# A router phase's first operations ahead of the weight loads, and the low parts of w1 and w2 behind its one-hot

## The chip, the cores and the metric

The kernel runs on one core of a Trainium2 chip (trn2). The core has a matrix engine (TensorE, PE in the rows), VectorE (DVE), ScalarE (ACT), GpSimd (POOL) and a queue engine, SyncE (SP), which here only issues transfers; all five run their own instruction lists in order and wait for one another through semaphores. The metric is the device time of one execution in microseconds, here the median of three runs.

## What is computed

Three stages, in float32, of which the reference is (cut):

```python
for t in range(S):                                   # attention with decay, 4 x 8 heads, 768 steps, 48 wide
    state = alpha[:, :, t, :, None] * state + einsum('bhd,bhe->bhde', k[:, :, t], v[:, :, t])
    y[:, :, t] = einsum('bhd,bhde->bhe', q[:, :, t], state)
x = y.transpose(0, 2, 1, 3).reshape(3072, 384)

logits = x @ w_gate                                  # 8 experts, 384 tokens for each
for idx in argsort(-logits.flatten()):               # greedy: best pair first
    tok, e = idx // 8, idx % 8
    if assigned[tok] >= 0 or counts[e] >= 384: continue
    assigned[tok] = e; counts[e] += 1
for e in range(8):
    out[assigned == e] = relu(x[assigned == e] @ w1[e]) @ w2[e]      # 384 -> 1024 -> 384

g = out @ w_gate2                                    # 384 -> 1536
result = (g * sigmoid(g) * (out @ w_val)) @ w_out    # 1536 -> 384
```

## The kernel before

**Stages.** First the attention, in chunks of the 768 steps, which leaves x in DRAM (`xd`). Then the router and the experts, interleaved. The router runs in 8 phases (`Router.phase`): each searches a threshold by rounds of comparisons and counting matmuls, gives the tokens to their best expert that still has room, and closes one expert, whose token numbers `idx` and whose number `iw` it leaves. The experts are done in the order in which the phases close them: "expert 5" below is the sixth to be closed, by phase 5. For one expert's 384 tokens, `moe1` multiplies by w1 (`ph`, L758), takes the ReLU (`hT`, L759 and L760), and multiplies by w2 (`px`, L770); `moe2` makes gate and value (L788), their product `pp` (L795), its two parts `pTa`, `pTb` (L796 on ScalarE, L797 on GpSimd); `outp` multiplies by the output weights (`po`, L805, three groups of 36 matmuls), copies each out of PSUM (`o`, L808, ScalarE) and scatters it to the output rows (L809, an indirect transfer issued by GpSimd).

**Two halves of a number.** Each factor is kept as a high and a low float16 part, and a product is three matmuls. The weights of an expert come as float32 by a transfer on SP's queue into one of three buffers `stage` (`split`, L700). ScalarE writes the high part (L701). The low part of w1 is made by VectorE (L705). For w2 ScalarE first scales `stage` in place (L703) and GpSimd then subtracts (L704). A `stage` buffer is free for a next transfer when its low part is made. `loadw` does three loads of w1 and four of w2.

**The tokens of an expert.** `gather` issues three indirect transfers on GpSimd (L712), which fetch 128 rows of `xd` each by `idx`, and three transposing transfers on SP's queue (L720) that turn them into `xT`.

**PSUM.** `po`, `ph` and `px` share one pair of buffers (tag "pa"), so a group of L758 can only start when the group two before it has been copied out.

**The order.** The experts' code and the router's are generators. After each piece of expert work a counted time `now` goes forward, and `advance()` lets the current phase write its next step when `now` has come to `due`. When a phase is at its end, `advance()` calls `loads()`, which calls `loadw` for the expert that was just closed, and the next phase is begun at a later call. A phase's first operations after that are VectorE's: `pen` (L444, a penalty on full experts), `lp` (L447), the maximum `m` (L449), two passes for ties, the one-hot `oh_t` (L457), and the comparisons `cmp` (L527); six counting matmuls on TensorE (L532) read `oh_t` and `cmp`, VectorE's `cs` (L542) reads their sum, and one matmul (L545) reads `cs`. The phase's last are three matmuls (L618), then on VectorE `eq` (L621), two `et` (L623), `row` (L624) and `idx` (L626).

The Tile framework takes the instructions in the order in which the code writes them, estimates when each could run, and sets each engine's list by that. A call of `behind(x, y)` (`add_manual_dep` with no semaphore) keeps x behind y in that list where both are on one engine, and lets x's estimated time count from y's. Before the change, `pen` is held behind `idx` (`self.after`), and in `loadw` `lo` holds the low parts behind `idx` for expert 0 alone.

Of the kernel before, what the change touches and what calls it, by code (L numbers as in the profile page):

```python
# [356 lines left out]
class Router:  # L357
# [75 lines left out]
    def phase(self, i):  # L433
# [4 lines left out]
        bt=lambda a: a[:,None,:].to_broadcast([128,8,24])  # L438
# [12 lines left out]
        w=P2.tile([128,8,24],F32,name="w",tag="w",bufs=1)  # L451
        b=P2.tile([128,24],F32,name="bw")
# [1 line left out]
        v.tensor_tensor(w,w,be(self.w8),op=OP.mult)  # L454
        v.tensor_reduce(b,w.rearrange("p e t -> p t e"),axis=X,op=OP.max)
        oh=oh_t.rearrange("p t e -> p e t")
        v.tensor_tensor(oh,w,bt(b),op=OP.is_equal)  # L457
        if not first:
            mu=P2.tile([128,24],F32,name="mu")
            v.tensor_tensor(mu,m,self.ua,op=OP.add)  # L460
# [7 lines left out]
        else:  # L468
            lo,hi=yield from self.search(m,oh_t,i)
# [214 lines left out]
def ffn(ctx, tc, xd, w1, w2, M, MW, out, R, side):  # L684
# [11 lines left out]
    def split(dst,src,scale,dma_after=None,lo_after=None,pool=False):  # L696

        n,w=src.shape[0]//128,src.shape[1]
        s=ST.tile([128,1024],F32,name="stage",tag="stage",bufs=3)[:,:n*w].rearrange("p (a b) -> p a b",a=n)
        behind(nc.sync.dma_start(s,src.rearrange("(a p) b -> p a b",p=128)),dma_after)  # L700
        nc.scalar.activation(dst[0],s,AF.Copy,scale=scale)  # L701
        if pool:
            nc.scalar.activation(s,s,AF.Copy,scale=scale)  # L703
            behind(nc.gpsimd.tensor_tensor(dst[1],s,dst[0],op=OP.subtract),lo_after)  # L704
        else: behind(nc.vector.scalar_tensor_tensor(dst[1],s,scale,dst[0],op0=OP.mult,op1=OP.subtract),lo_after)  # L705
    xT={}; mm=R.mm
    id16=R.id16
    def gather(e):
        xT[e]=W2.tile([128,6,3,128],F16,name="xT")
        for j in range(3):  # L710
            r=W2.tile([128,2*DM],F16,name="rows",tag="rows",bufs=3)
            last=nc.gpsimd.indirect_dma_start(out=r,out_offset=None,in_=xr,in_offset=bass.IndirectOffsetOnAxis(ap=IDX[e][:,0,j:j+1],axis=0))  # L712
            if e==0 and XP0:

                pt=PT.tile([128,6,128],F16,name="ptx",tag=("pg","pg","pv")[j],bufs=2)
                for c in range(6): mm(pt[:,c],lhsT=r[:,c*128:(c+1)*128],rhs=id16,is_transpose=True,start=c==0,stop=c==5,skip_group_check=True)
                nc.vector.tensor_copy(xT[e][:,0:XA,j],pt[:,0:XA])
                if XA<6: nc.scalar.activation(xT[e][:,XA:6,j],pt[:,XA:6],AF.Copy)
            else:
                last=nc.sync.dma_start_transpose(xT[e][:,:,j],r)  # L720
        return last
    W={}
    def warm():

        ps=PT.tile([128,CAP],F32,name="warm",tag="pa",bufs=PA)
        for i in range(NW): behind(mm(ps,lhsT=R.own[:,0:128],rhs=R.own,start=True,stop=True),R.lastp)
    def loadw(e):
        if e==0 and NW: warm()
        a=W2.tile([128,2,3,F1],F16,name="w1s"); b=W2.tile([128,2,8,DM],F16,name="w2s")
        lo=R.after if e==0 else None  # L730
        if e==0 and GF: g=lo=gather(e)
        ex=nc.values_load(IW[e],engines=[mybir.EngineType.SP],min_val=0,max_val=E-1,skip_runtime_bounds_check_because="the router gives numbers of experts")
        wa=w1[bass.ds(ex,1)].rearrange("e d f -> (e d) f"); wb=w2[bass.ds(ex,1)].rearrange("e f d -> (e f) d")
        if e<WH:

            for h in range(2):
                c=slice(512*h,512*h+512)
                for k in (slice(0,2),slice(2,3)): split((a[:,0,k,c],a[:,1,k,c]),wa[k.start*128:k.stop*128,c],64.0,None,lo,WP[e]&1)
                if h==0 and not (e==0 and GF): g=gather(e)
        else:  # L740
            for k in range(3):
                split((a[:,0,k:k+1],a[:,1,k:k+1]),wa[k*128:k*128+128],64.0,None,lo,WP[e]&1)
            g=gather(e)
        if e: lo=g=None
        for k in range(4):
            split((b[:,0,2*k:2*k+2],b[:,1,2*k:2*k+2]),wb[k*256:k*256+256],64.0,g,lo,WP[e]&2)
        W[e]=(a,b)
# [64 lines left out]
    now=[0.0]; ph=[0]; cur=[R.phase(0)]; due=[0.0]; loaded=[0]; freed=[0]; avail={}; loaded_at=[]  # L812
    def loads():
        while loaded[0] in R.res and loaded[0]<freed[0]+2:
            i=loaded[0]; IDX[i],IW[i]=R.res[i]
            loadw(i); loaded[0]+=1; avail[i]=now[0]+GL; loaded_at.append(now[0])
    def advance():
        try: due[0]=now[0]+next(cur[0])
        except StopIteration:
            loads(); ph[0]+=1; cur[0]=R.phase(ph[0]) if ph[0]<E else None; due[0]=now[0]  # L820
    def run(g):

        t=next(g,None)
        if t is None: return False
        now[0]+=t
        while cur[0] is not None and due[0]<=now[0]: advance()
        for _ in range(CV): next(side,None)
        return True
    M.step=CS>0
    while ph[0]<1:  # L830
        advance()
        for _ in range(CS): next(side,None)
# [4 lines left out]
    while due[0]<=0: now[0]=due[0]; advance()  # L837
# [70 lines left out]
```

## Time and profile before

| | us |
|---|---|
| three runs | 1011.41, 1005.70, 1004.32 |
| median | 1005.7 |
| profiled execution | 1007.58 |
| its span | 1005.8 |
| TensorE busy | 835.2 (83%) |
| VectorE busy | 682.2 (68%) |
| ScalarE busy | 415.7 (41%) |
| GpSimd busy | 325.2 (32%) |
| mean granted TensorE clock, of 1 | 0.929 |

The span is cut by the page into 40 slices of 25.1 us; each digit is an engine's busy share in tenths, and PEclk is the granted TensorE clock in tenths:

```profile
PE   1577687967517679799899989989989997999997
DVE  8999989649798998657746865764775676232130
POOL 0434333436206443503412241350351236121231
PEclk9779799997758789899999999999999999999999
```

The attention takes some 13 slices, the router's first phase follows, and the experts take the rest, from about 350 us on. A time in a row counts from the start of the span. A row of a timeline merges neighbours of one kind; its length runs from the first's start to the last's end, and the bracket at its end is the idle time of the engine ahead of it with what ended it.

### The profile page before, as it was taken

What the parts mean: (1) busy time and instruction counts of PE and PEld (TensorE: products, weight loads), DVE (VectorE), ACT (ScalarE), POOL (GpSimd) and SP (SyncE); (2) the same over time, 40 slices, a digit from 0 to 9 for tenths busy, and PEclk for the clock granted to TensorE, in tenths of its full rate; (3) what the DMA queues carried; (4) which work ended last, traced back from release to release, by engine and by line L of the source; (5) the groups of instructions that cost most, each with busy time, mean ns of one, the idle gap of its engine ahead of it and who ended that gap; (6) DMA issues with size and microseconds to landing.
All of it is one profiled execution on the core that took longest, in us unless ns stands there. A gap on an engine that the chain in (4) does not pass through costs nothing. (4 is left out here: it accounts for less than half of the span.)

```text
span 1005.8 us, 18465 instructions
## 1 busy us (share of the span) xinstructions
PE 835.2 (83%) x7216; PEld 532.4 (53%) x7216; DVE 682.2 (68%) x1856; ACT 415.7 (41%) x768; POOL 325.2 (32%) x308
## 2 busy tenths in 40 slices
PE   1577687967517679799899989989989997999997
PEld 0356566756414345456556556645655653566664
DVE  8999989649798998657746865764775676232130
ACT  5637465865406453413422332251342245332130
POOL 0434333436206443503412241350351236121231
PEclk9779799997758789899999999999999999999999
DMA  9985999969416430600520240050050038100000
GB/s 190 166 130 98 189 178 143 178 121 199 118 42 194 127 102 5 192 1 1 152 46 1 95 103 2 30 167 1 1 174 23 1 119 226 26 1 1 24 1 24
DMA packets 144215, 90.28 MB, mean 90 GB/s; under 512 B 120960, under 2 KB 133760, under 8 KB 144128
## 3 DMA queue, kind: packets, MB, share of 16 engines
q1 hardware_dynamic: 141056, 79.67, 36.2%
q0 software_dynamic: 3072, 9.44, 2.9%
q8 instruction: 56, 0.92, 0.4%
q14 instruction: 31, 0.25, 0.1%
HBM read 62.94 MB, written 9.44 MB: 72 GB/s over the span
## 5 line engine op out<-in xcount | busy, mean ns | idle before, releaser
L797 POOL TENSOR_TENSOR pTa<-pp,pTa 128x384 f16<-128x384 f32 x64 | 59.5, 930 | 270.3 <-ACT pTa L796 267.0
L758 PE MATMUL ph<-xT,w1s 128*128 128x384 f16 x576 | 102.7, 334 | 16.1 <-DMA xT<-rows 6.7
L805 PE MATMUL po<-ma,pTa 128*128 128x384 f16 x576 | 108.9, 339 | 0.7 <-ACT pTa L796 0.7
L792 DVE TENSOR_TENSOR sg<-sg,pg 128x384 f32<-128x384 f32 x96 | 52.6, 548 | 77.7 <-ACT sg L791 77.7
L770 PE MATMUL px<-hT,w2s 128*128 128x384 f16 x576 | 99.7, 331 | 5.4 <-DVE hT L760 5.0
L758 PEld LDWEIGHTS <-w1s 128*128 128x128 f16 x576 | 55.9, 100 | 54.5 <-issue 21.0
L770 PEld LDWEIGHTS <-w2s 128*128 128x128 f16 x576 | 56.5, 99 | 43.9 <-issue 8.9
L805 PEld LDWEIGHTS <-pTa 128*128 128x128 f16 x576 | 57.2, 101 | 40.0 <-issue 5.7
L788 PEld LDWEIGHTS <-mb 128*128 128x128 f16 x576 | 55.7, 99 | 39.1 <-issue 4.1
L788 PEld LDWEIGHTS <-mc 128*128 128x128 f16 x576 | 55.6, 98 | 36.4 <-issue 0.2
L788 PEld LDWEIGHTS <-ma 128*128 128x128 f16 x576 | 55.4, 98 | 35.7
L791 ACT ACTIVATE sg<-pg 128x384 f32<-128x384 f32 x96 | 46.5, 484 | 55.0 <-PE pg L788 54.5
L796 ACT ACTIVATE pTa<-pp 128x384 f16<-128x384 f32 x64 | 33.3, 522 | 85.5 <-DVE pp L795 85.5
L795 DVE SCALAR_TENSOR_TENSOR pp<-sg,pv 128x384 f32<-128x384 f32 x96 | 52.8, 551 | 17.4 <-PE pv L788 12.2
L704 POOL TENSOR_TENSOR w2s<-stage,w2s 128x768 f16<-128x768 f32 x32 | 53.6, 1685 | 25.8 <-ACT stage L703 25.5
L797 POOL TENSOR_TENSOR pTb<-pp,pTb 128x384 f16<-128x384 f32 x32 | 33.3, 1042 | 86.8 <-ACT pTb L796 86.8
L788 PE MATMUL pg<-x,mb 128*128 128x384 f16 x288 | 59.2, 333 | 2.1 <-DVE x L773 1.2
L210 POOL TENSOR_TENSOR vh<-vx,vh 128x384 f16<-128x384 f32 x24 | 23.7, 990 | 106.1 <-ACT vh L209 73.2
L265 POOL TENSOR_TENSOR sBD<-st,sBD 48x384 f16<-48x384 f32 x46 | 48.0, 1044 | 30.6 <-ACT sBD L264 28.8
L788 PE MATMUL pv<-x,mb 128*128 128x384 f16 x288 | 57.4, 326 | 0.0
L161 DVE TENSOR_TENSOR FG<-FG,al 96x192 f32<-96x192 f32 x124 | 55.2, 453 | 2.4
L760 DVE SCALAR_TENSOR_TENSOR hT<-ph,hT 128x384 f16<-128x384 f32 x64 | 34.9, 546 | 28.6 <-ACT hT L759 28.6
(246 smaller groups left out, 1884.1 us busy)
## 6 DMA issues: line engine op xcount, KB each, us to landing
stage<-in_moe_w_dram SPq DMA_DIRECT2D x32, 384.0 KB, 3.6
stage<-in_moe_w_dram SPq DMA_DIRECT2D x23, 512.0 KB, 4.4
al<-in_alpha_dram SPq DMA_DIRECT2D x16, 288.0 KB, 6.1
qx<-in_q_dram SPq DMA_DIRECT2D x16, 288.0 KB, 9.3
kx<-in_k_dram SPq DMA_DIRECT2D x16, 288.0 KB, 11.4
vx<-in_v_dram SPq DMA_DIRECT2D x64, 72.0 KB, 3.3
xd<-xr SPq DMA_DIRECT2D x24, 192.0 KB, 3.5
words<-in_moe_w_gate_dram SPq DMA_DIRECT2D x9, 512.0 KB, 4.0
```

The source lines that it names most:

```text
L161: chain[p]=nc.vector.tensor_tensor(fg(j,HB-1-j),fg(j-1,HB-j),aa(j,HB-j),op=OP.mult)
L265: (nc.vector if n>=NG-ND else nc.gpsimd).tensor_tensor(sb[r,1,:,h,0:D],s[r],sb[r,0,:,h,0:D],op=OP.subtract)
L704: behind(nc.gpsimd.tensor_tensor(dst[1],s,dst[0],op=OP.subtract),lo_after)
L758: mm(ps,lhsT=a[:,l,k,f*128:(f+1)*128],rhs=x[:,r,k],start=i==0,stop=i==8); i+=1
L760: nc.vector.scalar_tensor_tensor(hT[:,1,f],ps,0.0,hT[:,0,f],op0=OP.max,op1=OP.subtract)
L770: mm(ps,lhsT=b[:,l,f,d*128:(d+1)*128],rhs=hT[:,r,f],start=i==0,stop=i==23); i+=1
L788: mm(ps,lhsT=w[:,l,k,f%4*128:(f%4+1)*128],rhs=x2[:,r,k],start=i==0,stop=i==8); i+=1
L791: nc.scalar.activation(sg,pg,AF.Sigmoid,scale=2.0**-16)
L792: nc.vector.tensor_tensor(sg,sg,pg,op=OP.mult)
L795: nc.vector.scalar_tensor_tensor(p,sg,2.0**-13,pv,op0=OP.mult,op1=OP.mult)
L797: nc.gpsimd.tensor_tensor(pT[e][f//4][:,1,f%4],p,pT[e][f//4][:,0,f%4],op=OP.subtract)
L805: mm(po,lhsT=pT[e][f//4][:,l,f%4,t*128:(t+1)*128],rhs=M.o[f//4][:,r,f%4],start=i==0,stop=i==35); i+=1
```

## The change

From the end of phase 1 on, `advance()` begins the next phase at once and writes its first step (`pen` to `oh_t`, and the first `cmp`) ahead of `loads()`. The operation that writes `oh_t` is kept as `self.best`, and for experts 1 to 6 the low parts of w1 and now of w2 too are held behind it in their engine's list; for expert 7 (no phase follows) by nothing. `e` 0 is as it was. Lines of the changed kernel stand one lower than before from L730 on (L758 is L759, L805 is L806, L808 is L809), and four lower behind `advance`.

```diff
--- before.py
+++ after.py
@@ -454,7 +454,7 @@
         v.tensor_tensor(w,w,be(self.w8),op=OP.mult)
         v.tensor_reduce(b,w.rearrange("p e t -> p t e"),axis=X,op=OP.max)
         oh=oh_t.rearrange("p t e -> p e t")
-        v.tensor_tensor(oh,w,bt(b),op=OP.is_equal)
+        self.best=v.tensor_tensor(oh,w,bt(b),op=OP.is_equal)
         if not first:
             mu=P2.tile([128,24],F32,name="mu")
             v.tensor_tensor(mu,m,self.ua,op=OP.add)
@@ -727,7 +727,8 @@
     def loadw(e):
         if e==0 and NW: warm()
         a=W2.tile([128,2,3,F1],F16,name="w1s"); b=W2.tile([128,2,8,DM],F16,name="w2s")
-        lo=R.after if e==0 else None
+
+        lo=R.after if e==0 else R.best if e<E-1 else None
         if e==0 and GF: g=lo=gather(e)
         ex=nc.values_load(IW[e],engines=[mybir.EngineType.SP],min_val=0,max_val=E-1,skip_runtime_bounds_check_because="the router gives numbers of experts")
         wa=w1[bass.ds(ex,1)].rearrange("e d f -> (e d) f"); wb=w2[bass.ds(ex,1)].rearrange("e f d -> (e f) d")
@@ -741,7 +742,7 @@
             for k in range(3):
                 split((a[:,0,k:k+1],a[:,1,k:k+1]),wa[k*128:k*128+128],64.0,None,lo,WP[e]&1)
             g=gather(e)
-        if e: lo=g=None
+        if e: g=None
         for k in range(4):
             split((b[:,0,2*k:2*k+2],b[:,1,2*k:2*k+2]),wb[k*256:k*256+256],64.0,g,lo,WP[e]&2)
         W[e]=(a,b)
@@ -817,7 +818,10 @@
     def advance():
         try: due[0]=now[0]+next(cur[0])
         except StopIteration:
-            loads(); ph[0]+=1; cur[0]=R.phase(ph[0]) if ph[0]<E else None; due[0]=now[0]
+            if ph[0]==0: loads()
+            ph[0]+=1; cur[0]=R.phase(ph[0]) if ph[0]<E else None; due[0]=now[0]
+            if cur[0] is not None and ph[0]>1: due[0]+=next(cur[0])
+            loads()
     def run(g):
 
         t=next(g,None)
```

**VectorE at expert 5**, from the last `pp` of expert 4 on. Names are those of the program; `r_` is a PSUM tile of the router. Before:

```order
L705 SCALAR_TENSOR_TENSOR w1s<-stage,w1s 128x1024
L621 TENSOR_TENSOR eq<-r_9791,q_4322 128x72
L623 TENSOR_TENSOR et<-eq,pay 128x72 x2
L705 SCALAR_TENSOR_TENSOR w1s<-stage,w1s 128x1024
L624 TENSOR_REDUCE row<-et 128x6
L705 SCALAR_TENSOR_TENSOR w1s<-stage,w1s 128x1024
L626 TENSOR_TENSOR idx<-row,r_9791 128x6
L444 TENSOR_SCALAR pen<-full 128x8
...
L457 TENSOR_TENSOR oh_t<-w,bw 128x8x24
L542 TENSOR_TENSOR cs<-r_9975,blk 128x32
```

After:

```order
L621 TENSOR_TENSOR eq<-r_9791,q_4322 128x72
L623 TENSOR_TENSOR et<-eq,pay 128x72 x2
L624 TENSOR_REDUCE row<-et 128x6
L626 TENSOR_TENSOR idx<-row,r_9791 128x6
L444 TENSOR_SCALAR pen<-full 128x8
...
L457 TENSOR_TENSOR oh_t<-w,bw 128x8x24
L705 SCALAR_TENSOR_TENSOR w1s<-stage,w1s 128x1024 x3
L542 TENSOR_TENSOR cs<-r_9928,blk 128x32
```

The three low parts of w1 stood between the operations that give `idx`, ahead of `pen`; now they stand together behind `oh_t`, ahead of `cs`.

**SP's queue at expert 5**, from the first load of w1 to the last of w2 (rows named ISA left out; the numbers tell the buffers' uses apart: the fourth use of `stage` takes the first's buffer, and so on). Before:

```order
L700 DMA stage_9909<-in_moe_w1_dram 128x1024
L700 DMA stage_9913<-in_moe_w1_dram 128x1024
L700 DMA stage_9917<-in_moe_w1_dram 128x1024
L700 DMA stage_9931<-in_moe_w2_dram 128x2x384
L700 DMA stage_9936<-in_moe_w2_dram 128x2x384
L700 DMA stage_9941<-in_moe_w2_dram 128x2x384
L720 DMA_TRANSPOSE xT_9921<-rows_9922 128x6x128
L720 DMA_TRANSPOSE xT_9921<-rows_9925 128x6x128
L720 DMA_TRANSPOSE xT_9921<-rows_9928 128x6x128
L700 DMA stage_9946<-in_moe_w2_dram 128x2x384
```

After:

```order
L700 DMA stage_9938<-in_moe_w1_dram 128x1024
L700 DMA stage_9942<-in_moe_w1_dram 128x1024
L700 DMA stage_9946<-in_moe_w1_dram 128x1024
L720 DMA_TRANSPOSE xT_9950<-rows_9951 128x6x128
L720 DMA_TRANSPOSE xT_9950<-rows_9954 128x6x128
L700 DMA stage_9960<-in_moe_w2_dram 128x2x384
L720 DMA_TRANSPOSE xT_9950<-rows_9957 128x6x128
L700 DMA stage_9965<-in_moe_w2_dram 128x2x384
L700 DMA stage_9970<-in_moe_w2_dram 128x2x384
L700 DMA stage_9975<-in_moe_w2_dram 128x2x384
```

The first two transposes now stand ahead of the first load of w2 and the third ahead of the second; before, all three stood ahead of the fourth.

**ScalarE at expert 5**, between the last high part of w1 and the first `hT`; `o_10017`, `o_10067` and `o_10133` are the copies of expert 4's three `po`. Before:

```order
L701 ACTIVATE w2s_9905<-stage_9931 128x768
L703 ACTIVATE stage_9931<-stage_9931 128x768
L808 ACTIVATE o_10017<-po_9980 128x384
L701 ACTIVATE w2s_9905<-stage_9936 128x768
L703 ACTIVATE stage_9936<-stage_9936 128x768
L701 ACTIVATE w2s_9905<-stage_9941 128x768
L703 ACTIVATE stage_9941<-stage_9941 128x768
L808 ACTIVATE o_10067<-po_10020 128x384
L701 ACTIVATE w2s_9905<-stage_9946 128x768
L703 ACTIVATE stage_9946<-stage_9946 128x768
L808 ACTIVATE o_10133<-po_10070 128x384
L759 ACTIVATE hT_10136<-ph_10137 128x384
```

After:

```order
L809 ACTIVATE o_10017<-po_9980 128x384
L701 ACTIVATE w2s_9934<-stage_9960 128x768
L703 ACTIVATE stage_9960<-stage_9960 128x768
L809 ACTIVATE o_10067<-po_10020 128x384
L701 ACTIVATE w2s_9934<-stage_9965 128x768
L701 ACTIVATE w2s_9934<-stage_9970 128x768
L703 ACTIVATE stage_9965<-stage_9965 128x768
L703 ACTIVATE stage_9970<-stage_9970 128x768
L701 ACTIVATE w2s_9934<-stage_9975 128x768
L703 ACTIVATE stage_9975<-stage_9975 128x768
L809 ACTIVATE o_10133<-po_10070 128x384
L760 ACTIVATE hT_10136<-ph_10137 128x384
```

The first copy moved ahead of the first load of w2, the second ahead of the second; the third stands behind the fourth in both.

On TensorE at experts 2 to 5 the six matmuls of L532 stand 12 matmuls of `po` earlier: behind the first three on `pTb` of the second group of `po`, where before they stood behind the first three on `pTa` of the third. L545 stands 21 matmuls behind them in both, and L758 follows after the last of `po`. On GpSimd the three gathers stand ahead of all low parts of w2 and all stores in both kernels. Behind them came before: low part, store, two low parts, store, low part, store; now: store, low part, store, three low parts, store. At expert 1 the row behind the gathers is now two stores, two low parts, store, two low parts; at expert 6 two stores, three low parts, store, low part.

## Rows read from the trace of the kernel before

**Rows 1.** Windows of 20 us: length, busy time (x instructions) by engine, PEclk, DMA, GB/s
```profile
core 0: us, PE busy (x) PEld busy (x) DVE busy (x) ACT busy (x) POOL busy (x), PEclk, DMA share, GB/s
...
740.00:760.00 20.00, 17.02 (x106) 9.73 (x106) 12.59 (x34) 8.95 (x14) 12.53 (x10) 0.91 0.58 159
```
**Rows 2.** List of waits: who waits for whom, us in all, times, longest us
```profile
PE r L532 <- DVE oh_t L457: 12.3, 4, 3.4
...
PE ph L758 <- DVE hT L760: 6.6, 7, 3.2
```
**Rows 3.** Timeline of TensorE, 735 to 762: start, length, instruction, [idle before, releaser]
```profile
736.07 0.23 PE L618 MATMUL r<-S,ownl 128*128 128x26 f16 x3
...
749.33 0.32 PE L532 MATMUL r<-oh_t,cmp 128*128 128x32 f16 x6 [2.98 <-DVE oh_t L457]
749.49 5.25 PE L805 MATMUL po<-ma,pTa 128*128 128x384 f16 x21
...
756.56 1.63 PE L758 MATMUL ph<-xT,w1s 128*128 128x384 f16 x9
...
758.10 1.62 PE L758 MATMUL ph<-xT,w1s 128*128 128x384 f16 x9
```
**Rows 4.** Timeline of TensorE, the same 21 matmuls at experts 2, 3 and 4
```profile
500.45 5.25 PE L805 MATMUL po<-ma,pTa 128*128 128x384 f16 x21
...
583.89 4.77 PE L805 MATMUL po<-ma,pTa 128*128 128x384 f16 x21
...
666.98 3.57 PE L805 MATMUL po<-ma,pTa 128*128 128x384 f16 x21
```
**Rows 5.** Timeline of VectorE, 736 to 770
```profile
737.94 1.22 DVE L705 SCALAR_TENSOR_TENSOR w1s<-stage,w1s 128x1024 f16<-128x1024 f32 x1 [1.73 <-ACT w1s L701]
...
742.64 0.16 DVE L444 TENSOR_SCALAR pen<-full 128x8 f32<-128x8 f32 x1
...
746.13 3.14 DVE L457 TENSOR_TENSOR oh_t<-w,bw 128x192 f16<-128x192 f32 x1
```
**Rows 6.** Timeline of VectorE, 815 to 865, the same instruction at expert 6
```profile
828.82 1.03 DVE L457 TENSOR_TENSOR oh_t<-w,bw 128x192 f16<-128x192 f32 x1
```
**Rows 7.** Timeline of GpSimd, 736 to 770
```profile
738.40 1.54 POOL L797 TENSOR_TENSOR pTb<-pp,pTb 128x384 f16<-128x384 f32 x1 [2.85 <-ACT pTb L796]
742.99 1.06 POOL L712 DMA_INDIRECT rows<-xd,idx  x1 [3.06 <-DVE pen L444]
744.36 1.11 POOL L712 DMA_INDIRECT rows<-xd,idx  x1 [0.30 <-issue]
...
746.74 1.65 POOL L704 TENSOR_TENSOR w2s<-stage,w2s 128x768 f16<-128x768 f32 x1
```
**Rows 8.** View of the tile `rows`, 740 to 760: the three gathers' transfers
```profile
DMA to landing us min/median/max: 2.9/3.3/4.9
```
**Rows 9.** Timeline of SP's queue, 736 to 770
```profile
747.91 4.01 SPq L720 DMA_TRANSPOSE xT<-rows  x3
752.13 0.42 SPq L700 DMA_DIRECT2D stage<-in_moe_w_dram  x1
```
**Rows 10.** Timeline of ScalarE, 736 to 770
```profile
755.54 0.84 ACT L701 ACTIVATE w2s<-stage 128x768 f16<-128x768 f32 x1 [5.40 <-DMA stage<-in_moe_w_dram]
...
757.22 0.47 ACT L808 ACTIVATE o<-po 128x384 f32<-128x384 f32 x1
```
**Rows 11.** The page, part 6: DMA issues, KB each, median us to landing
```profile
stage<-in_moe_w_dram SPq DMA_DIRECT2D x32, 384.0 KB, 3.6
```
**Rows 12.** Timeline of TensorE at experts 1 (400 to 430) and 6 (835 to 845)
```profile
403.61 0.23 PE L618 MATMUL r<-S,ownl 128*128 128x26 f16 x3
...
422.59 4.71 PE L758 MATMUL ph<-xT,w1s 128*128 128x384 f16 x18 [6.71 <-DMA xT<-rows]
...
840.58 1.62 PE L758 MATMUL ph<-xT,w1s 128*128 128x384 f16 x9 [0.84 <-ACT o L808]
```
**Rows 13.** Timeline of GpSimd, 840 to 855, a gather of expert 7
```profile
847.73 1.37 POOL L712 DMA_INDIRECT rows<-xd,idx  x1 [0.30 <-issue]
```

## The prediction, made before the changed kernel was run

> **What bounds the kernel now.** I read the 20 us windows first, then the list of waits, then one boundary engine by engine. In the stage of the experts TensorE is what takes the time: it stops only where one expert's work gives way to the next. In the slice 740 to 760 it is busy 17.02 of 20 us at a mean granted clock of 0.91 [rows 1]. The list of waits names the stop: four times, 12.3 us in all, at most 3.4, TensorE stands at L532 because VectorE has not finished `oh_t`, the one-hot of the next router phase [rows 2]. In the boundary in front of expert 6 (expert 5 was just routed; I call each boundary by the expert whose weights are loaded in it) the six matmuls of L532 start at 749.33 after 2.98 us of idling, and the next 21 take 5.25 us [rows 3]; the same 21 take 4.77 us at expert 3 and 3.57 us at expert 4 [rows 4]. That is the granted clock falling to its lower level, 1.2 GHz, for a stretch behind the idle time: 1.68, 1.20 and 0 us lost, and at expert 2 once more 1.68. So the four boundaries (experts 2 to 5) cost 12.3 + 4.6 = 16.9 us. The reader is to see in [rows 3] that nothing else waits there: L758 follows at 756.56 and its second group at 758.10 without a gap.
>
> Why `oh_t` is late is on VectorE [rows 5]: it stands idle 1.73 us for the first low part of w1, does three low parts of 1.22 us between the operations that give `idx`, and then needs 742.64 to 746.13 to come to `oh_t`, which takes 3.14 us. At expert 6 the same instruction takes 1.03 us [rows 6]; the difference is the low part of w2 on GpSimd, 746.74 to 748.39 [rows 7], which it overlaps.
>
> **The change at one boundary (expert 5).** VectorE is free at 737.94 - 1.73 = 736.21, and the input of `eq` is there at 736.07 + 0.23 = 736.30 [rows 3, 5]. From the first low part to `pen` it takes 742.64 - 737.94 = 4.70 us, of which three low parts are 3.66; so `pen` comes at 736.30 + 1.04 = 737.35, `oh_t` starts 3.49 later at 740.8 and ends, at 1.03 us, at 741.9 instead of 749.27. TensorE came to L532 at 749.33 - 2.98 = 746.35; now 12 matmuls fewer stand ahead of it, at 3.57/21 = 0.17 us, so it comes at 744.3 and does not wait (2.4 us to spare). The low parts follow to 741.9 + 3.66 = 745.5, then `cs`. Its user, L545, stands 21 matmuls behind L532, at 744.6 + 3.57 = 748.2: no wait, 2.7 us to spare. TensorE would then begin L758 at 756.56 - 2.98 - 1.68 = 751.9.
>
> The gathers wait for `idx` and for GpSimd's last `pTb`, which ends at 738.40 + 1.54 = 739.9 [rows 7]: they start at 740.0, 741.4 and 742.75 instead of 742.99, 744.36 and later, and land after 3.3 us [rows 8], so the second is there at 744.7. The two transposes that now stand ahead of the first load of w2 on SP's queue (1.34 us each, 4.01/3) [rows 9] end at 746.0.
>
> **What is late next.** ScalarE works in its written order. Its copy `o` of the third `po` frees the PSUM buffer for the second group of L758, and it stands behind the fourth load of w2 in both kernels. Before, that load was issued at 752.13 [rows 9], its high part ran at 755.54, `o` at 757.22 [rows 10], done at 757.69: 0.4 us ahead of the 758.10 at which TensorE came. So the cover was thin. Now: the first load of w2 goes out at 746.1 (its buffer, freed by the first low part at 743.1, is not the later one), lands after 3.6 us [rows 11] at 749.7; high part and scaling take 757.22 - 755.54 = 1.68, to 751.4; the low part on GpSimd 1.65, to 753.05; that frees the buffer of the fourth load, which lands 755.54 - 752.13 = 3.41 later, at 756.5; again 1.68, then 0.47: `o` is done at 758.7. The second group of L758 starts at 758.7, 0.6 us later than before, though the first was ready at 751.9 and ended at 753.4. **The wait of 2.98 us at L532 is replaced by one of 5.3 us at L758.** The transposes (third landing near 750) and the first group's buffer (copy near 751.9) just keep up. Four boundaries of the same rows: 4 x 0.6 = +2.4.
>
> The bounds of this chain: with landings of 2.9 everywhere [rows 8] it ends 1.6 earlier, with 4.9 at the first gather and both loads 4.5 later. So -1.0 to +5.1 each. Coming together at all four they would be -4 to +20; I take -4 to +8, since 3.3 and 3.6 are medians.
>
> The clock: an idle stretch of 5.3 us is nearest to the 6.71 us at expert 1, behind which 18 matmuls took 4.71 us [rows 12] against 18 x 0.17 = 3.06, so 1.6 us lost each, 6.4 against 4.6 now: +1.8 (bounds -4.6 and +2.2).
>
> **The two boundaries that differ.** Expert 1: TensorE waits 6.71 us for `xT` [rows 12]. From L618's end at 403.84 the same offsets give `pen` at 404.95, gathers from 405.3, `oh_t` to 409.5, transposes issued 408.6 to 413.2, landing by 415.4, before TensorE comes at 422.59 - 6.71 = 415.88. There `o` of the third `po` stands behind the third load only: loads at 411.4, 413.3, 413.8 give `o` done at 419.9, and the two first groups end at 421.6 instead of 427.3. The fourth load then stands ahead of the second `hT` (about 1 us), and the clock may fall (1.6 at most): -3.5, between -5.7 and -1. Expert 6, with the last phase behind it: two of GpSimd's stores go ahead of the first low part of w2, and the same chain ends near 841.6 against 840.58 [rows 12], +1.0; but the waits for `hT` that follow there (most of 6.6 us) [rows 2] come from loads ahead of `hT` on ScalarE and VectorE, and in the new order the first `hT` goes ahead of w1's. I take 2.7 back: -1.7, between -4 and +2.
>
> **The sum.** +2.4 + 1.8 - 3.5 - 1.7 = -1.0. The profiled execution took 1007.58 us, of which 1005.8 are its span; it would take 1006.6. The median of the three runs shown is 1.9 lower, so 1005.7 - 1.0 = 1004.7.
>
> **Rivals.** *The full gain.* The copies come in time after all, and all 16.9 us of the four boundaries, some 4 at expert 1 and 3 at expert 6 are given back: 1005.7 - 24 = 982. For it speaks that the list of waits names `oh_t` alone; against it that `o` had 0.4 us to spare and the fourth load is issued 1 us later than before. To gain 10 us, each of the four chains would have to be 2.5 us shorter than I make it.
>
> *The gathers are held by the low parts (slower).* Three low parts in a row stand beside the second and third gather on GpSimd. One gather of expert 7 beside a low part took 1.37 us [rows 13] against 1.06 [rows 7], so 0.3 us. If instead they were held until the last low part's end at 745.5, the second would land at 748.8 and the second transpose end at 750.1, 4.1 us later, with all that hangs on it: 4 x 4.1 and about 4 at each of the other two, some 24 us, 1029. It decides from about 2 us per boundary. The Trainium skill (SBUF — State Buffer, section Who interferes with whom, and its box on DMAs issued by GpSimd) says that VectorE and GpSimd share a port pair as an exclusive lock, and that descriptors can't be written while VectorE runs in a two-port mode. For an instruction with two SBUF inputs outside those modes, as a low part is, it names only reads of GpSimd as held. By the first sentence this rival's 1029 would come out, by the second none of it; the row of 1.37 us is on the side of the second.
>
> *The low parts make `cs` late.* They end at 745.5, L545 comes at 748.2. Even 5 us more would end inside the wait for `o`, so it gives no time of its own.
>
> **How the numbers follow.** Forecast (the wait moves to L758, the sum within some 9 us of none): 0.74. Full gain or most of it: 0.16. Gathers held, or long landings at all boundaries: 0.10. A change of 1%, 10 us, is about what a measurement of this kernel can tell from none. Faster by over 1% is the first rival, 0.16; slower is the last, 0.10; the rest 0.74. The range goes from the forecast's lower bounds taken together (-4 - 2 - 3 = -9 to -10) to +8, rounded: 995 to 1013. I leave 0.12 below and 0.07 above.
>
> **What would show it.** In the changed kernel's trace: `oh_t` at about 1.03 us and no wait at L532; the low parts directly behind it; a wait of 4 to 6 us of L758 for ScalarE's `o` at experts 2 to 5, with the fourth load of w2 ending last before it; the 6.71 us for `xT` gone; the second group of L758 at expert 5 about 22 us behind L618, as before. It is wrong if that wait is under 2 us (then the full gain), or if the gathers take over 2 us.

## The result

The changed kernel is slower. Its median was 1019.45 us (1013.44 to 1022.89) against 1005.01 (1002.25 to 1011.41), a ratio of 1.0132 with a 95% interval of 1.0092 to 1.0171. A second series of five rounds gave 1018.49 against 1007.74, 1.0104 (1.0076 to 1.0132): 10 to 13 us, a little over 1%. The profiled execution took 1021.76 us, its span is 1020.0.

The page of the changed kernel, its first part (busy time, share of the span, instructions) and the granted clock:

```profile
PE 841.4 (82%) x7216; PEld 536.8 (53%) x7216; DVE 667.5 (65%) x1856; ACT 415.0 (41%) x768; POOL 324.7 (32%) x308
...
PEclk9769799897758789899989999989999998999999
```

The engines have hardly more to do than before (TensorE is busy 6 us more, VectorE 15 less); the span grew by waiting. The list of waits has no row for L532 and `oh_t` any more, against the 12.3 us of [rows 2], and a new one:

```profile
PE ph L759 <- ACT o L809: 32.3, 11, 5.5
```

TensorE at expert 5, the boundary that the prediction worked out:

```profile
747.38 0.23 PE L618 MATMUL r<-S,ownl 128*128 128x26 f16 x3
...
755.41 0.30 PE L532 MATMUL r<-oh_t,cmp 128*128 128x32 f16 x6
...
764.13 1.62 PE L759 MATMUL ph<-xT,w1s 128*128 128x384 f16 x9 [1.07 <-ACT o L809]
765.59 0.30 PE L532 MATMUL r<-oh_t,cmp 128*128 128x32 f16 x6
770.97 3.04 PE L759 MATMUL ph<-xT,w1s 128*128 128x384 f16 x9 [5.08 <-ACT o L809]
773.80 0.23 PE L545 MATMUL r<-cs,G 128*128 128x32 f16 x1
773.88 3.34 PE L759 MATMUL ph<-xT,w1s 128*128 128x384 f16 x18
```

This answers [rows 3]. The row L618 is the end of a router phase, from which I count; a group of L759 is nine matmuls. L532 no longer waits. L759 (L758 of before) begins 16.75 us behind L618 instead of 20.49, and then its second group stands for 5.08 us until `o` is done, and runs 3.04 us where nine matmuls otherwise take 1.62: from 771 to 774 us the granted clock was 0.50, its lower level of 1.2 GHz. The group starts 23.59 us behind L618, before 22.03. The granted clock fell from 1.00 to 0.91 between the two slices in which this lies (the same columns as [rows 1]):

```profile
740.00:760.00 20.00, 20.00 (x134) 12.10 (x132) 16.77 (x49) 5.70 (x10) 7.50 (x8) 1.00 0.55 142
760.00:780.00 20.00, 13.86 (x86) 7.89 (x85) 7.24 (x33) 9.62 (x15) 8.48 (x6) 0.91 0.34 106
```

Why L532 no longer waits is on VectorE at the same place (answering [rows 5]): the one-hot and, directly behind it, the three low parts of w1.

```profile
752.71 1.01 DVE L457 TENSOR_TENSOR oh_t<-w,bw 128x192 f16<-128x192 f32 x1
753.34 3.69 DVE L705 SCALAR_TENSOR_TENSOR w1s<-stage,w1s 128x1024 f16<-128x1024 f32 x3
```

The chain of the new wait stands on three engines. SP's queue (answering [rows 9]):

```profile
753.88 4.06 SPq L720 DMA_TRANSPOSE xT<-rows  x2
758.20 0.40 SPq L700 DMA_DIRECT2D stage<-in_moe_w_dram  x1
...
760.19 5.63 SPq L700 DMA_DIRECT2D stage<-in_moe_w_dram  x3
```

ScalarE, the first and the fourth high part of w2 and what follows (answering [rows 10]):

```profile
761.94 0.84 ACT L701 ACTIVATE w2s<-stage 128x768 f16<-128x768 f32 x1 [9.37 <-DMA stage<-in_moe_w_dram]
...
768.77 0.84 ACT L701 ACTIVATE w2s<-stage 128x768 f16<-128x768 f32 x1 [0.89 <-DMA stage<-in_moe_w_dram]
769.70 0.84 ACT L703 ACTIVATE stage<-stage 128x768 f32<-128x768 f32 x1
770.45 0.47 ACT L809 ACTIVATE o<-po 128x384 f32<-128x384 f32 x1
```

GpSimd, the gathers and the first low part of w2 (answering [rows 7]):

```profile
750.72 0.98 POOL L712 DMA_INDIRECT rows<-xd,idx  x1
752.01 0.97 POOL L712 DMA_INDIRECT rows<-xd,idx  x1 [0.30 <-issue]
753.28 0.95 POOL L712 DMA_INDIRECT rows<-xd,idx  x1 [0.30 <-issue]
...
763.79 1.63 POOL L704 TENSOR_TENSOR w2s<-stage,w2s 128x768 f16<-128x768 f32 x1 [8.16 <-ACT stage L703]
```

The first load of w2 goes out behind two transposes at 758.20, its data are there at 761.94, GpSimd's low part ends at 765.42 and frees the buffer, the fourth load, the last of the row of three, goes out at 765.45, its data are there at 768.77, and only then, behind two more passes, comes `o`.

**Where the 10 us lie.** For each boundary I took the start of the second and of the eighth group of L759 (L758 before) behind the L618 ahead of them, in both traces. In us, before and after:

| expert | second group | eighth group | difference of the eighth |
|---|---|---|---|
| 1 | 21.81, 18.50 | 31.75, 30.53 | -1.2 |
| 2 | 22.60, 24.80 | 32.22, 35.85 | +3.6 |
| 3 | 21.71, 23.64 | 31.32, 34.27 | +3.0 |
| 4 | 22.12, 22.94 | 31.73, 33.83 | +2.1 |
| 5 | 22.03, 23.60 | 31.64, 34.24 | +2.6 |
| 6 | 21.18, 22.71 | 37.45, 37.76 | +0.3 |

Together +10.4; expert 0 gives -0.2. The other 4.0 us of the 14.2 between the two spans lie ahead of the first L618 (302.92 and 306.95), where both kernels have the same instructions.

### The profile page after: what moved, and what is told of

It reads as the page before. It is cut to its first block, busy times and chain, and to the rows that moved or that the text cites. A ratio compares the mean times of both kernels' runs of the same rounds, so it can differ in the third digit from the quotient of the medians.

```text
span 1020.0 us, 18469 instructions
## 1 busy us (share of the span) xinstructions
PE 841.4 (82%) x7216; PEld 536.8 (53%) x7216; DVE 667.5 (65%) x1856; ACT 415.0 (41%) x768; POOL 324.7 (32%) x308
## 5 line engine op out<-in xcount | busy, mean ns | idle before, releaser
L759 PE MATMUL ph<-xT,w1s 128*128 128x384 f16 x576 | 111.6, 352 | 39.6 <-ACT o L809 32.3
L806 PE MATMUL po<-ma,pTa 128*128 128x384 f16 x576 | 103.9, 329 | 0.7 <-ACT pTa L797 0.7
L759 PEld LDWEIGHTS <-w1s 128*128 128x128 f16 x576 | 58.1, 104 | 84.4 <-issue 54.3
L806 PEld LDWEIGHTS <-pTa 128*128 128x128 f16 x576 | 55.7, 98 | 37.4 <-issue 1.2
L796 DVE SCALAR_TENSOR_TENSOR pp<-sg,pv 128x384 f32<-128x384 f32 x96 | 52.8, 551 | 17.4 <-PE pv L789 12.2
L265 POOL TENSOR_TENSOR sBD<-st,sBD 48x384 f16<-48x384 f32 x46 | 48.6, 1056 | 32.0 <-ACT sBD L264 30.2
L798 POOL TENSOR_TENSOR pTb<-pp,pTb 128x384 f16<-128x384 f32 x32 | 30.3, 946 | 86.7 <-ACT pTb L797 86.7
L210 POOL TENSOR_TENSOR vh<-vx,vh 128x384 f16<-128x384 f32 x24 | 23.4, 979 | 107.7 <-ACT vh L209 72.3
```

The lines of the kernel that those rows point to most:

```text
L265: (nc.vector if n>=NG-ND else nc.gpsimd).tensor_tensor(sb[r,1,:,h,0:D],s[r],sb[r,0,:,h,0:D],op=OP.subtract)
L759: mm(ps,lhsT=a[:,l,k,f*128:(f+1)*128],rhs=x[:,r,k],start=i==0,stop=i==8); i+=1
L796: nc.vector.scalar_tensor_tensor(p,sg,2.0**-13,pv,op0=OP.mult,op1=OP.mult)
L798: nc.gpsimd.tensor_tensor(pT[e][f//4][:,1,f%4],p,pT[e][f//4][:,0,f%4],op=OP.subtract)
L806: mm(po,lhsT=pT[e][f//4][:,l,f%4,t*128:(t+1)*128],rhs=M.o[f//4][:,r,f%4],start=i==0,stop=i==35); i+=1
```

## Experiments

Each edit is to the changed kernel unless it says otherwise. The eighth group's place behind L618 is given for experts 2, 3, 4 and 5 (before 32.2, 31.3, 31.7, 31.6; changed 35.9, 34.3, 33.8, 34.2), and the ratio is to the kernel before on the same chip.

**e1: the reorder alone**

```diff
-        lo=R.after if e==0 else R.best if e<E-1 else None
+        lo=R.after if e==0 else None
```

> The changed kernel, but no low part is held behind the one-hot for experts 1 to 7; only the next phase's first segment is written ahead of the loads. On the engines the low parts of w1 stand again between the operations that give idx, and the transposes again behind three loads of w2. Theory A (the 10 us come from the place of the low parts behind the one-hot, through the stage buffers, w2's fourth load and ScalarE's copy o): as the kernel before, 1005 us within 4; waits of about 3 us at L532 back, the eighth group of L759 31.6 to 32.2 us behind L618 at experts 2 to 5 (changed kernel 33.8 to 35.9), no wait of 5 us at L759. Rival B (writing the phase ahead of the loads costs the time by itself): 1015 us or more, the eighth group at 33.8 or later.

0.9998 (0.9968 to 1.0027), 1005.17 us; eighth group at 31.8, 31.7, 31.5, 31.0. VectorE at expert 5, the last low part of w1 and the one-hot:

```profile
738.70 1.21 DVE L705 SCALAR_TENSOR_TENSOR w1s<-stage,w1s 128x1024 f16<-128x1024 f32 x1
743.39 3.14 DVE L457 TENSOR_TENSOR oh_t<-w,bw 128x192 f16<-128x192 f32 x1
```

TensorE there:

```profile
746.59 0.32 PE L532 MATMUL r<-oh_t,cmp 128*128 128x32 f16 x6 [2.99 <-DVE oh_t L457]
```

The wait at L532 is back, and the loss is gone. Writing the phase ahead of the loads costs and brings nothing; the 10 us come with the place of the low parts and with the order on SP's queue that follows from it (here the transposes stand behind three loads of w2 again). What w1's and w2's place each do was not run apart. Rival B is out.

**e2: four buffers**

```diff
-        s=ST.tile([128,1024],F32,name="stage",tag="stage",bufs=3)[:,:n*w].rearrange("p (a b) -> p a b",a=n)
+        s=ST.tile([128,1024],F32,name="stage",tag="stage",bufs=4)[:,:n*w].rearrange("p (a b) -> p a b",a=n)
```

> The changed kernel with four buffers stage instead of three. The fourth load of w2 then takes a buffer that VectorE's low part of w1 frees, not the one that GpSimd's first low part of w2 frees, and the first load of w2 has a buffer at once and stands ahead of the transposes. Theory A (the second group of L759 waits for o, o for the fourth load's high part, the load for GpSimd's first low part): the second group about 20.3 us behind L618 instead of 23.6 at expert 5, its wait for o 1.5 to 2 us instead of 5.1, some 3.3 us and some of the clock saved at each of experts 2 to 6: 1000 us within 5. Rival C (the fourth load is late for SP's queue, behind the transposes, not for its buffer): the wait stays over 4 us, 1012 us or more.

0.9966 (0.9939 to 0.9993), 1002.03 us. At expert 5 the second group starts 20.35 us behind L618, after a short wait, and at the full clock:

```profile
752.56 1.62 PE L759 MATMUL ph<-xT,w1s 128*128 128x384 f16 x9 [2.22 <-ACT o L809]
```

The eighth group: 32.5, 28.4, 30.7, 29.5, up to 6 us earlier. But the edit takes away two links at once, as SP's queue shows at expert 5: the fourth load no longer needs the buffer that GpSimd's low part frees, and the first load of w2 (the last of the row of four) now stands ahead of the transposes.

```profile
729.41 2.53 SPq L700 DMA_DIRECT2D stage<-in_moe_w_dram  x4
738.71 3.82 SPq L720 DMA_TRANSPOSE xT<-rows  x2
```

So this run alone does not part the buffer from the place of the transposes (rival C); e7 does. Two more things were not foreseen: at expert 2 a wait of 3.75 us stayed, and at expert 0, whose loads use the buffers too and so got another order, the distance from the first to the second L618 grew from 100.5 to 105.2 us.

**e3: zeros in the wait**

```diff
-            i=0
+            i=0; Z=NZ if f==0 and 1<e<6 else 0
...
+            for z in range(Z): mm(ps,lhsT=zero,rhs=x[:,0,0],start=False,stop=z==Z-1)
```

`zero` is a tile of zeros and `NZ` is 28, so the sums in `ps` stay what they are.

> The changed kernel, with 28 matmuls that add zeros (weights zero) at the end of the first group of L759 at experts 2 to 5, some 4.6 us of TensorE work laid into the wait of 5.1 us. It adds work and leaves none out. Theory A with the clock (the second group runs at the lower granted clock because TensorE idled ahead of it, 3.04 instead of 1.62 us, and the loss comes on top of the wait): the second group still about 23.6 us behind L618 at expert 5, but its length 1.62, the eighth group 1.0 to 1.4 us earlier at each of the four; 4 to 6 us faster than the changed kernel in the profile. Rival D (the length of 3.04 is a wait for weights or for the copies, not the clock): the group stays near 3 us, no gain or some us lost.

1.0027 (1.0001 to 1.0053), 1007.44 us, 8 to 11 us faster than the changed kernel (by the two series of that) with 112 matmuls more. TensorE at expert 5:

```profile
752.68 4.71 PE L761 MATMUL ph<-xT,zero 128*128 128x384 f16 x28
757.23 0.30 PE L532 MATMUL r<-oh_t,cmp 128*128 128x32 f16 x6
757.80 1.62 PE L760 MATMUL ph<-xT,w1s 128*128 128x384 f16 x9 [0.27 <-ACT o L811]
```

The second group runs in 1.62 instead of 3.04 us at all four. From its start to that of the eighth it is 9.14 to 9.15 us here, 11.05, 10.63, 10.89 and 10.64 in the changed kernel: the clock costs it 1.5 to 1.9 us a boundary, 6.6 in all. Rival D is out, for these groups hang on the same weights and copies. The gain is larger than expected because the chain too was shorter in this execution at three of the four (second group 23.4, 22.5, 23.5, 22.1).

**e4: four buffers as in e2, and the transposes behind the last load `d` of w2**

```diff
-            else:
-                last=nc.sync.dma_start_transpose(xT[e][:,:,j],r)
+            else: late.setdefault(e,[]).append(r)
...
+            if e and k==3:
+                for j,r in enumerate(late[e]): behind(nc.sync.dma_start_transpose(xT[e][:,:,j],r),d)
```

> The changed kernel with four buffers stage and with the three transposes of each expert but the first written behind all four loads of w2 on SP's queue. Theory A: the loads of w2 go out as the low parts of w1 end (7, 8.3, 9.6 us behind L618), the last high part is done near 16, o at once when po is done, so the second group of L759 follows the first without a wait over 1 us, near 17.5 to 18.5 us behind L618, the eighth near 27; 5 to 7 us less than the changed kernel at each of experts 2 to 6, 985 to 992 us, faster than the kernel before. Rival E (the transposes are then too late and the first group waits for xT): a wait of over 2 us for xT ahead of the first group, 1000 us or more.

0.9899 (0.9856 to 0.9943), 997.44 us: faster than the kernel before, but 5 us above what was expected. The eighth group stands at 30.9, 28.4, 28.4, 28.2, 5 to 6 us earlier than in the changed kernel (5 to 7 were expected, and a place near 27), and at expert 5 the second group follows the first without a wait:

```profile
751.87 1.62 PE L761 MATMUL ph<-xT,w1s 128*128 128x384 f16 x9 [1.72 <-ACT o L811]
753.49 1.62 PE L761 MATMUL ph<-xT,w1s 128*128 128x384 f16 x9
```

Expert 0 took the missing 5 us (105.7 between its two L618, as in e2), and at expert 2 the transposes were late (4.37 us for `xT`).

**e5 and e6: an extra buffer for the first load of w2 alone, transposes last, on the changed kernel and on the kernel before**

```diff
-        s=ST.tile([128,1024],F32,name="stage",tag="stage",bufs=3)[:,:n*w].rearrange("p (a b) -> p a b",a=n)
+        s=(ST.tile([128,1024],F32,name="stage",tag="stagex",bufs=1) if x else ST.tile([128,1024],F32,name="stage",tag="stage",bufs=3))[:,:n*w].rearrange("p (a b) -> p a b",a=n)
```

Here `x` is true for the first load of w2 of the experts from 1 on; the transposes stand as in e4.

> The changed kernel with the transposes written behind all four loads of w2 for experts 1 to 7, and with one more buffer that only the first load of w2 of these experts takes; expert 0 keeps its three buffers. Theory A: at experts 3 to 5 as with four buffers for all (eighth group 28.2 to 28.4 us behind L618, changed kernel 33.8 to 34.3), and the distance between the first two L618, 105.7 us there, back at 100.5: 992 us within 4. Rival: expert 0 is slow there for another reason than its own buffers, 997 us.

> The kernel before with the same two edits (extra buffer for the first load of w2, transposes behind the loads of w2), without the change itself. Theory A (the change takes away 3 us of waiting and up to 1.7 us of clock at four boundaries, which the loads of w2 take back): here the waits of 3 us at L532 stay, the eighth group at 31 to 32 us behind L618, 1003 to 1007 us, so 10 to 15 us behind the changed kernel with the same edits. Rival F (the change itself is worth nothing, the two edits alone bring the gain): the same time as that kernel within 3 us, 992 us or so.

On the changed kernel 0.9888 (0.9855 to 0.9921), 995.61 us, the fastest median of all, though not apart from e4's within the intervals; on the kernel before 0.9999 (0.9979 to 1.0018), 1006.26. So the two edits bring nothing by themselves, and the change brings 1.1% once they are there: what it gives at L532 is real, and the loads of w2 had taken it. Rival F is out. Expert 0 is back at 100.1. The eighth group is at 30.7, 30.4, 30.2, 30.4, some 2 us later than expected, because now the first group waits for `xT` and the clock falls there. TensorE in e5 at expert 5:

```profile
751.16 2.60 PE L761 MATMUL ph<-xT,w1s 128*128 128x384 f16 x9 [2.33 <-DMA xT<-rows]
```

In e6 the wait of before stays, TensorE at expert 5:

```profile
751.78 0.32 PE L532 MATMUL r<-oh_t,cmp 128*128 128x32 f16 x6 [2.99 <-DVE oh_t L457]
```

**e7: transposes behind the third load, three buffers**

```diff
+            if e and k==2:
+                for j,r in enumerate(late[e]): behind(nc.sync.dma_start_transpose(xT[e][:,:,j],r),d)
```

The rest of the edit to the transposes is that of e4; there is no fourth buffer.

> The changed kernel with three buffers as it has, and the transposes written behind the third load of w2, where the kernel before has them. The fourth load still takes the buffer that GpSimd's first low part of w2 frees, but that low part comes about 2.5 us earlier since the first load of w2 no longer stands behind two transposes. Theory A: second group of L759 19 to 20.5 us behind L618 at expert 5 (23.6 in the changed kernel), 1000 us within 5. Rival C2 (the place of the transposes does not matter for the chain): 22.5 or later, 1012 us or more.

0.9938 (0.9914 to 0.9963), 1000.60 us; the second group at 20.4 us at expert 5 as expected, the eighth at 30.5, 30.7, 29.5, 30.3. TensorE, SP's queue and GpSimd at expert 5:

```profile
747.53 1.62 PE L761 MATMUL ph<-xT,w1s 128*128 128x384 f16 x9 [2.21 <-ACT o L811]
...
737.33 4.13 SPq L749 DMA_TRANSPOSE xT<-rows  x3
743.14 0.38 SPq L700 DMA_DIRECT2D stage<-in_moe_w_dram  x1
...
740.75 2.37 POOL L704 TENSOR_TENSOR w2s<-stage,w2s 128x768 f16<-128x768 f32 x1 [5.34 <-ACT stage L703]
```

This parts the two links of e2. Two transposes ahead of the first load are worth some 3 us of the chain at experts 3 to 5, so rival C2 is out. And the buffer is a link of its own: the fourth load still goes out only at 743.14, when GpSimd's first low part has ended (743.12), 1.7 us after the queue was done with the last transpose (741.46).

**e8: the copy `o` on VectorE**

```diff
-            nc.scalar.activation(o,po,AF.Copy,scale=2.0**-25)
+            nc.vector.tensor_scalar(o,po,2.0**-25,None,op0=OP.mult)
```

> The changed kernel with the copy o made by VectorE instead of ScalarE, nothing else. Theory A (ScalarE's written order holds the copy and the first hT behind the fourth load of w2): the wait for o is gone and the second group follows the first at about 17.3 us behind L618, but the first hT still stands behind the fourth load's high part and scaling, so the third group waits some 5 us in its place and starts near 24.2 instead of 26.5: some 2 us saved per boundary, 1006 to 1011 us. Rival G (it is enough that PSUM is copied out elsewhere): no wait over 2 us in front of the third group, 995 us or less.

1.0062 (1.0038 to 1.0087), 1013.03 us. The wait for `o` is gone and the next thing behind the fourth load, the first `hT`, makes the third group wait instead. TensorE at expert 5:

```profile
759.87 1.62 PE L759 MATMUL ph<-xT,w1s 128*128 128x384 f16 x9
766.21 5.64 PE L759 MATMUL ph<-xT,w1s 128*128 128x384 f16 x18 [4.70 <-DVE hT L761]
```

It starts 23.5 us behind L618 (expected 24.2), but at the lower clock (18 matmuls in 5.64 us against 3.08), so the eighth group stands at 33.8, 34.0, 34.2, 33.5: of the 2 us expected at each of these four, only expert 2 kept them, and the time is above the 1006 to 1011 expected. Rival G is out.

**e9, e10 and e12: three more ways out, each short of what was expected**

e9 moves the fourth load of w2 behind the second group and its two passes on ScalarE behind the second `hT`; e10 adds the transposes of e7; e12 is e5 with the transposes behind the second load.

```diff
+            if e and k==3: D4[e]=S; continue
...
-            nc.scalar.activation(hT[:,0,f],ps,AF.Relu)
+            h0=nc.scalar.activation(hT[:,0,f],ps,AF.Relu)
...
+            if f==1 and e in D4: D4[e](h0)
```

(`S` is the call of `split`, which holds the two passes behind `h0`; in e12 the `k==3` of e4 is `k==1`.)

> The changed kernel with one move: the fourth load of w2 of experts 1 to 7 is written in moe1 behind the second group of L759, and its high part and scaling stand behind the second hT on ScalarE, so the third copy o no longer stands behind them. Transposes and buffers stay. Theory A (o stands behind the fourth load on ScalarE): o is done right behind the third load's scaling, 20.2 us behind L618 at expert 5 instead of 23.6, the second group starts there, its wait 1.5 to 2.2 us instead of 5.1 and short enough that the clock mostly stays: 3 to 5 us less at each of experts 2 to 6, 1000 us within 5. Rival H (the wait has another end than the fourth load, the third load or the first hT at the same time): the wait stays over 4 us, 1012 or more.

> The changed kernel with the fourth load of w2 behind the second group of L759 as in the run before, and with the transposes written behind the third load of w2; three buffers. Theory A: the third load's scaling ends near 16.5 us behind L618, xT is there near 16.4, so neither o nor xT makes a wait of 2 us; the second group near 18, the eighth near 27 to 28.5 (changed kernel 33.8 to 35.9), 990 us within 4, the fastest of all. Rival E (xT is late, and behind a wait of over 2 us the clock falls as with the extra buffer): the eighth group near 30.3, 996 us.

> The changed kernel with the extra buffer for the first load of w2 and with the transposes behind the second load of w2 instead of the fourth. Theory A: the transposes go out as soon as the gathers have landed, end near 12 us behind L618, so the first group of L759 starts at 15.6 without a wait for xT (18 with the transposes last); the last two loads of w2 follow at once, their high parts and scalings end near 18.5, so o makes the second group start near 19 with a wait under 2 us and no fall of the clock; the eighth group near 28.5 (30.4 with the transposes last), 990 to 995 us. Rival (the two loads behind the transposes land late, as the fourth does in the changed kernel): a wait of over 3 us for o, the clock falls, 1000 us or more.

e9: 1.0006 (0.9984 to 1.0029), 1007.99 us; eighth group 34.8, 30.7, 33.5, 32.7. e10: 0.9919 (0.9890 to 0.9948), 1001.04; 32.4, 31.2, 34.0, 29.7. e12: 0.9957 (0.9931 to 0.9983), 1003.26; 33.4, 30.6, 32.9, 31.0. In e9 the second group came at 20.56 us at expert 5, close to the 20.2 expected, so `o` did stand behind the fourth load; but its 3.42 us of waiting still lowered the clock, and the two passes now stood between two `hT`. TensorE in e9 at expert 5:

```profile
760.19 2.42 PE L761 MATMUL ph<-xT,w1s 128*128 128x384 f16 x9 [3.42 <-ACT o L812]
...
767.65 1.62 PE L761 MATMUL ph<-xT,w1s 128*128 128x384 f16 x9 [1.08 <-DVE hT L763]
```

Those 1.68 us on ScalarE have no free place between groups of 1.5 us: in e10 a later group waits 1.75 us for `hT` at each of experts 2 to 5, and at experts 2 and 4 the first group waits 2.4 and 2.5 us (rival E in part). In e12 the rival decided: the loads behind the transposes were late, and the second group waited 2.6 to 4.6 us for `o`.

**e11: the changed kernel again**

> The changed kernel once more, unaltered, for a closer interval. In the two profiles the experts' part (from the first L618 on) is 10.2 us longer than in the kernel before, and 4.0 us lie ahead of it, where both kernels have the same instructions. If those 4 us are scatter between executions: a ratio near 1.010, and the first L618 somewhere between 300 and 307 us. If they belong to the change: 1.014 or more, the first L618 again near 307.

1.0104 (1.0076 to 1.0132). The first L618 stands at 301.49 us, the eighth group at 35.2, 34.3, 33.9, 34.1. The loss at the boundaries came again, the 4 us ahead of them did not; over all fourteen profiles the first L618 lies between 300.40 and 306.95, whatever the kernel. They are scatter.

## Why the prediction was wrong

The forecast was 1004.7, in a range to 1013.0; the slow side had 0.10, for held gathers, which did not come, or for long landings at all boundaries, which came at some. It named the mechanism of the four boundaries and got its cost wrong. In the sum -1.0 was forecast and +10.4 measured; two steps failed most: the chain was priced with the landings of the old order (+2.4, measured +6.5), and the clock term took off a loss that its starting point already held (+1.8, measured +4.8).

- **No wait at L532, `oh_t` at 1.03 us:** right. It took 1.01 us at expert 5 and ended 6.3 us behind L618 (forecast 5.8). No wait for `cs` at L545 either, as forecast.
- **The wait moves to the second group of L758 (now L759), for `o` behind the fourth load:** right, 5.08 us at expert 5 where 5.3 was written, 4.6, 5.2 and 5.2 at experts 2 to 4. That 5.08 comes so close to 5.3 is in part luck: the first group began 0.9 us later than forecast (it waited 1.07 us for the second `o`, of which the prediction said that it just keeps up), and the second 1.0 later. e7 and e9 each took away one link of the chain and shortened the wait, e2 and e4 took away two; e8 took away its end, and the wait moved to the next user.
- **The chain, +2.4 for four boundaries:** too short. The second group came 2.2, 1.9, 0.8 and 1.6 later, +6.5, within the bounds given but far from the value taken. At expert 5 the second transpose started 4.7 us behind the start of its gather, not 3.3 (it is the last 1.2 us of the row that ends at 757.94). At experts 2 and 3 the first load took 5.7 and 5.1 us to its high part instead of the median of 3.6. The medians were those of the old order, in which that load went out with no transpose just ahead of it; but at experts 4 and 5 it took 3.5 and 3.7 in the new order too, so why it was slow at the other two is not shown. SP's queue in the changed kernel at expert 2, that load:

```profile
499.37 0.40 SPq L700 DMA_DIRECT2D stage<-in_moe_w_dram  x1
```

ScalarE there:

```profile
505.02 0.84 ACT L701 ACTIVATE w2s<-stage 128x768 f16<-128x768 f32 x1 [10.06 <-DMA stage<-in_moe_w_dram]
```

- **The clock, +1.8:** here the working itself failed. The loss behind the wait was sized well (1.6 each, 6.4; e3 shows 6.6). But the 4.6 us that the clock cost before were taken off it, and they lie ahead of the second group: the 758.10 of [rows 3], with which the new start was compared, already holds them. They were given back twice. What is to come off is only 1.8 us for the four (0.46 each: 9.61 from the second to the eighth group before, 9.15 in e3): router matmuls that stood between the groups and now stand in the wait, and a short wait behind them. So +4.8 instead of +1.8.
- **Expert 1, -3.5:** -1.2. `o` was done 18.5 us behind L618 (407.43 there) instead of 16.3, so the second group began at 18.5 and at the lower clock, and ended at 21.5 instead of the 18.0 that the forecast's 421.6 means. The second load of w2 went out at 12.2 us instead of 9.7, behind the third transpose, which started 5.8 us behind the start of its gather (3.3 assumed); the first load took 5.0 us to its high part (3.6 assumed). Either alone would have held `o` within 0.3 us of there, for the second high part stood idle only 0.28 us for its data. In e11 the place of the eighth group gives -0.9. SP's queue, then ScalarE, at expert 1:

```profile
418.16 1.22 SPq L720 DMA_TRANSPOSE xT<-rows  x1
419.65 5.13 SPq L700 DMA_DIRECT2D stage<-in_moe_w_dram  x3
...
422.94 0.84 ACT L701 ACTIVATE w2s<-stage 128x768 f16<-128x768 f32 x1 [0.28 <-DMA stage<-in_moe_w_dram]
```

- **Expert 6, -1.7:** +0.3. The second group came 1.5 us later (forecast 1.0), and the waits for `hT` behind it gave back 1.5 us instead of 2.7: they were 3.23 and 2.26 before, and are 1.04, 1.28 and 1.64 now. The lower clock was left out on both sides, and that did not matter: behind the wait of 5.52 us 27 matmuls took 6.37 us, and before, behind that of 3.23 us, 45 took 9.15, some 1.7 to 1.8 us lost in each.
- **The rivals:** the gathers were not held until the last low part's end. At experts 3 to 5 they took 0.95 to 0.99 us; at expert 5 two were over before the first low part began at 753.34, and the third, which began just ahead of it at 753.28, took 0.95. One that began inside a low part took longer, 1.97 us at expert 2 and 1.23 at expert 6, still under the 2 us that the prediction set, and its low parts went on for 1.4 us and more after it. Of what the prediction weighed from the Trainium skill (SBUF — State Buffer, section Who interferes with whom, and its box on DMAs issued by GpSimd), the 0.95 us agrees with the sentence that names only reads of GpSimd as held by an instruction like a low part; what the 1.0 us more at expert 2 was, the rows do not tell. The full gain did not come; e5 and e6 put the change at about 11 us where the loads are out of the way, half of the 24 that this rival had.
- **The chances:** a sum of four small terms, each with its own bounds, got 0.74 for staying within 10 us. All four missed on the same side. They share transfers and the clock, so they were not four independent terms; I had added their bounds on the low side and cut them on the high side.

## What to carry to other kernels

When a wait is taken off the path, ask what else the instructions moved past free: here the low parts free the load buffers, and a copy that stands behind a load on ScalarE freed PSUM with 0.4 us to spare. A new chain is to be priced with the landing times of the order that it will run in, and against one fixed point: a loss that lies ahead of that point in the old trace must not be taken off again. And a wait costs more than its length where the granted clock falls behind it (5.1 us of waiting cost some 1.5 more).

## What was not expected of the hardware

Whether the clock falls is not told by the length of the idle time alone. In the kernel before nothing was lost behind the longest wait, 3.4 us at expert 4 [rows 2, 4], and behind 2.98 it was once 1.2 us and twice 1.68; behind 2.22 us in e2 and behind 2.69 us in e7 (expert 3) nine matmuls took 1.62 us, behind 2.33 us in e5 2.60. Longer waits had it each time: ahead of the second group at experts 2 to 6 TensorE stood for 4.6 to 5.5 us in the two profiles of the changed kernel, ten times, and each time that group took 2.9 to 3.0 us. So one more wait of 2 or 3 us has no fixed price. That this is part of why e5, e10 and e12, alike on paper, differ by up to 8 us is likely, but was not run apart.
